# A second substitution on VectorE, held loads, and expert 1's splits on GpSimd

## The chip, the cores and the metric
The kernel runs on one core of one Trainium2 chip. The metric is the device time of one execution in microseconds (us). The engines are named as in the profile: PE is TensorE, DVE is VectorE, ACT is ScalarE, POOL is GpSimd, and SP issues most of the DMAs.

## What is computed
Two layers run behind each other: a delta-rule attention, and a mixture of eight experts on its output. Cut to what matters:

```python
# attention: B=4 batches, H=8 heads, S=768 tokens, D=48
k_n = k / (norm(k) + 1e-6); state = 0
for t in range(S):
    y[:,:,t] = q[:,:,t] @ state
    v_old    = k_n[:,:,t] @ state
    state   += beta[:,:,t] * outer(k_n[:,:,t], v[:,:,t] - v_old)
# experts: x = y as (4, 768, 384), E=8, F=1024
for each batch, token s:
    fresh = argmax(x[s] @ w_gate)
    e = fresh if s == 0 or sigmoid(x[s] @ w_local) < 0.5 else the expert of token s-1
    out[s] = softmax(x[s] @ w_gate)[e] * (relu(x[s] @ w1[e]) @ w2[e])
```

## The kernel before
**Attention.** The 768 tokens are cut into 12 chunks of 64, and two chunks make a macro m (six of them). The recurrence inside a chunk is turned into matrix products and one triangular inverse. `K(n)` loads keys and queries of chunk n (`KQ`, buffers of the pool W) and makes the Gram products in four groups on PE into two PSUM tiles (`pt`). Each group is evacuated by ACT and DVE (L208 to L211) into `gt` (one buffer for the whole kernel, the input of the inverse), `G2` (four buffers) and `amp`.

`T_(m)` makes the inverse for a macro. DVE prepares it: transposes of `gt` into L (L218), norms, and scaling of L in two halves (L232). Then comes the **substitution**: 31 steps, in each a product `fg<-L,X` (L241) and a subtraction `X<-X,fg` (L242), of (31-j)(j+1) elements on each of 128 partitions. All 31 steps of all six macros run on POOL. At the end DVE transposes X into TT (L249) and TX (L252). L and X have two buffers each, TT and TX one.

`Tc(n)` uses the inverse for chunk n: a product of TT with G2 on PE, its copy QQ (L264), a product of QQ with TX, and the matrix XT, which ACT writes in parts (L258, two copies of half the partitions each at L272, and L273). It also loads the values `kv` (768 KB a chunk, three buffers) and DVE scales them (L276). `online(n)` carries the state from chunk to chunk: products on PE with evacuations between them, the output y (L313), its store to HBM and a DMA transpose, and the product with the gate's weights, which ends in the logits `lg` (L326, L330).

**Experts.** `Moe` finds the expert of each token in two routings, z=0 over the first SP=20 of 24 steps, z=1 over the rest; each is a chain of small DVE operations with a few matmuls between. Token lists then gather rows of `xs` by indirect DMAs on POOL. Expert 0 runs in two pieces, the first with LOT=256 tokens from z=0. Weights are split into two f16 parts: the high part on ACT (`whi`, L431), the low one on DVE (`wlo`, L433) or, if the planner chooses so, on POOL by two operations. `weights` does this for experts 0 and 1 in the planned part, `rest` for the others in an order written out by hand. Up products (L448), down products (`downm`, L455), and for each tile of up to 128 tokens a scaling (`yo`, L456) and a scatter to the output follow.

**What sets the order.** Each operation of the attention, the routing and experts 0 and 1 is registered with `add(...)`, with what it reads and writes, the engines that may run it (`e=`) and a cost in ns (`c=`). `Sched` then puts the operations in one order by list scheduling: it takes the ready operation with the longest chain behind it, and a buffer of a pool is given in the order in which the buffers were asked for. What is late on the chip doesn't change this order, as each engine works its list from top to bottom. `boost` raises the priority of operations; `links` lets an operation count as if it waited for another one, for its priority alone; `pre` is a true predecessor.

Of the kernel before, what the change touches and what calls it, by code (L numbers as in the profile page):

```python
# [120 lines left out]
class Attn:  # L121
# [37 lines left out]
    def build(s,extra=(),pre={},post=None):  # L159
# [27 lines left out]
        def K(n):
# [3 lines left out]
            for g in range(2):  # L191
                for j in range(2): add(lambda g=g,j=j:nc.sync.dma_start(KQ[g].t[D(j)].rearrange("r a t -> r (a t)"),s.kq_[n,g,j]),p=[KQ[g]],e='S',c=196608); s.kl[n]=S.ops[-1]; S.ops[-1].pre.update([s.kl[1]] if n==2 else ())
            if cc==0:
                M["b"]=s.bt(); M["gt"]=s.gt()
                add(lambda:nc.sync.dma_start(M["b"].t,s.beta[m]),w=[M["b"]],e='S',c=16384)
            gt=M["gt"]
            for g in range(2):
                for c in range(2):
# [696 lines left out]
```

## Time and profile before

| | us |
|---|---|
| median of three runs | 585.5 (584.71 to 587.43) |
| the profiled execution's own time | 586.47 |
| its span | 584.8 |
| PE busy in it | 459.1 |
| DVE busy | 329.3 |
| POOL busy | 285.9 |
| ACT busy | 210.6 |

The span runs from the first to the last instruction that the profiler saw; the execution's own time includes what lies around it. Busy shares are means over stages that are bound by different engines, so they are read by stage. In a row of a timeline stand the start, the duration, the engine, the line, the operation and its tiles, and in brackets how long the engine had been idle and which engine's work ended that.

### The profile page before, as it was taken

What the parts mean: (1) busy time and instruction counts of PE and PEld (TensorE: products, weight loads), DVE (VectorE), ACT (ScalarE), POOL (GpSimd) and SP (SyncE); (2) the same over time, 40 slices, a digit from 0 to 9 for tenths busy, and PEclk for the clock granted to TensorE, in tenths of its full rate; (3) what the DMA queues carried; (4) which work ended last, traced back from release to release, by engine and by line L of the source; (5) the groups of instructions that cost most, each with busy time, mean ns of one, the idle gap of its engine ahead of it and who ended that gap; (6) DMA issues with size and microseconds to landing.
All of it is one profiled execution on the core that took longest, in us unless ns stands there. A gap on an engine that the chain in (4) does not pass through costs nothing. (4 is left out here: it accounts for less than half of the span.)

```text
span 584.8 us, 18802 instructions
## 1 busy us (share of the span) xinstructions
PE 459.1 (79%) x8119; PEld 351.9 (60%) x8119; DVE 329.3 (56%) x722; ACT 210.6 (36%) x346; POOL 285.9 (49%) x492
## 2 busy tenths in 40 slices
PE   4660277788998887985863489999999999999992
PEld 4550267787987887885862357545565555555551
DVE  3656226547448458233486834852858685868550
ACT  2330254454644755535313211520505141426110
POOL 4089888888888897882001421032233232322301
PEclk9999999577577598586555579999999999999997
DMA  8990001624654455453056372351474656575300
GB/s 224 215 188 1 0 3 58 161 46 129 165 106 106 142 147 165 86 112 57 4 110 244 79 157 94 117 179 48 123 200 126 171 172 174 152 213 151 90 13 25
DMA packets 63668, 69.47 MB, mean 119 GB/s; under 512 B 42931, under 2 KB 54255, under 8 KB 63584
## 3 DMA queue, kind: packets, MB, share of 16 engines
q1 hardware_dynamic: 60032, 58.20, 39.6%
q0 software_dynamic: 3552, 10.06, 5.7%
q8 instruction: 64, 1.05, 0.8%
q14 instruction: 20, 0.16, 0.1%
HBM read 49.49 MB, written 10.05 MB: 102 GB/s over the span
## 5 line engine op out<-in xcount | busy, mean ns | idle before, releaser
L242 POOL TENSOR_TENSOR X<-X,fg 128x31 f32<-128x31 f32 (+15 forms) x186 | 109.8, 590 | 14.6
L241 POOL TENSOR_TENSOR fg<-L,X 128x31 f32<-128x31 f32 (+15 forms) x186 | 98.4, 529 | 16.0 <-DVE X L231 1.6
L167 PE MATMUL pt<-W 48*64 48x128 f32 x768 | 64.1, 374 | 22.6 <-DVE gt L210 13.6
L167 PEld LDWEIGHTS pt<-W 48*64 48x64 f32 x768 | 55.3, 193 | 27.3 <-DVE gt L210 16.3
L448 PEld LDWEIGHTS <-W 128*128 128x128 f16 x432 | 43.7, 102 | 33.4 <-issue 6.9
L448 PE MATMUL pt<-kv,W 128*128 128x384 f16 (+3 forms) x288 | 61.5, 346 | 0.9 <-DVE ft L450 0.7
L450 DVE TENSOR_SCALAR ft<-pt 128x384 f32<-128x384 f32 (+6 forms) x72 | 40.1, 557 | 22.6 <-ACT W L449 14.6
L167 PE MATMUL pt<-TT,G 32*32 32x32 f32 x768 | 24.3, 229 | 31.8 <-DVE TT L249 30.8
L211 DVE TENSOR_TENSOR amp<-pt,mask 128x256 f32<-128x256 f32 x48 | 20.2, 422 | 50.1 <-ACT gt L208 30.9
L449 ACT ACTIVATE W<-pt 128x256 f16<-128x256 f32 (+4 forms) x28 | 12.2, 437 | 85.5 <-PE pt L448 84.1
L167 PEld LDWEIGHTS pt<-TT,G 32*32 32x32 f32 x768 | 22.5, 139 | 33.0 <-issue 27.2
L433 DVE SCALAR_TENSOR_TENSOR W<-W,W 128x768 f16<-128x768 f32 (+1 forms) x33 | 35.9, 1093 | 10.1 <-ACT W L431 9.9
L455 PEld LDWEIGHTS <-W 128*128 128x128 f16 (+2 forms) x272 | 28.0, 103 | 21.9 <-issue 6.4
L438 POOL DMA_INDIRECT out_dram<-y,so x9 | 11.2, 1246 | 55.2 <-DVE y L456 52.8
L436 POOL DMA_INDIRECT G<-xs,gi x25 | 26.6, 1066 | 22.2 <-PE pt L612 12.6
L167 PE MATMUL kps<-R,xtp 64*64 64x48 f32 x704 | 35.6, 281 | 0.7 <-issue 0.7
L449 ACT ACTIVATE xtp<-pt 128x384 f16<-128x384 f32 (+4 forms) x28 | 14.7, 526 | 56.0 <-PE pt L448 43.9
L167 PEld LDWEIGHTS kps<-R,xtp 64*64 64x64 f32 x704 | 34.4, 200 | 0.9 <-issue 0.7
L431 ACT ACTIVATE W<-W 128x768 f16<-128x768 f32 (+1 forms) x33 | 30.2, 935 | 10.7 <-DMA W<-in_moe_w_dram 8.2
L208 ACT ACTIVATE gt<-pt,ma 128x128 f32<-128x128 f32 x48 | 22.4, 479 | 27.1 <-PE pt L167 18.6
L438 POOL DMA_INDIRECT out_dram<-kf,so x7 | 7.9, 1124 | 49.1 <-DVE kf L456 27.0
L455 PEld LDWEIGHTS <-amp 128*128 128x128 f16 (+2 forms) x224 | 22.6, 101 | 14.6 <-issue 0.9
(307 smaller groups left out, 944.1 us busy)
## 6 DMA issues: line engine op xcount, KB each, us to landing
W<-in_moe_w_dram SPq DMA_DIRECT2D x24, 512.0 KB
W<-in_moe_w_dram SPq DMA_DIRECT2D x28, 384.0 KB
W<-in_kq_dram SPq DMA_DIRECT2D x48, 192.0 KB
kv<-in_kv_dram SPq DMA_DIRECT2D x12, 768.0 KB
xs<-y SPq DMA_DIRECT2D x48, 96.0 KB
amp<-in_moe_w_dram SPq DMA_DIRECT2D x3, 384.0 KB
G<-xs,gi POOLq DMA_INDIRECT x25
kv<-G SPq DMA_TRANSPOSE x25
```

Source lines behind the costliest of these rows:

```text
L167: mm=lambda o,l,r,st,sp,tp:MM(o,l,r,start=st,stop=sp,skip_group_check=True,tile_position=tp)
L208: add(lambda go=go,gv=gv:nc.scalar.activation(go(),gv()[:,:,0:32],AF.Copy,scale=s.ma[:,0:1]),r=[ps,"mask"],w=[key],claim=[gt],e='A',c=ca(128))
L211: add(lambda gv=gv,n0=n0:nc.vector.tensor_tensor(am.t[:,n0:n0+4,:],gv()[:,:,64:128],s.mask.unsqueeze(1).to_broadcast([128,4,64]),op=ALU.mu ...
L241: eng.tensor_tensor(tv,l[:,j,j+1:].unsqueeze(2).to_broadcast([128,n,k]),x[:,j,x0:x1].unsqueeze(1).to_broadcast([128,n,k]),op=ALU.mult)
L242: eng.tensor_tensor(x[:,j+1:,x0:x1],x[:,j+1:,x0:x1],tv,op=ALU.subtract)
L431: if e in (None,s.nc.scalar): s.nc.scalar.mul(o,i,256.0)
L433: def wlo(s,st,w,k): s.nc.vector.scalar_tensor_tensor(s.wv(w,k)[:,1],s.wst(st,k),256.0,s.wv(w,k)[:,0],op0=ALU.mult,op1=ALU.subtract)
L436: return s.nc.gpsimd.indirect_dma_start(out=x[0:m],out_offset=None,in_=s.xs[0:nt,:],in_offset=bass.IndirectOffsetOnAxis(ap=ix[0:m],axis=0) ...
L448: for k in range(3): s.nc.tensor.matmul(ps,s.wv(W[k],k)[:,a,0,128*f:128*f+128],xT[:,3*b+k,:],start=(x==0 and k==0),stop=(x==2 and k==2))
L449: def uphi(s,h,ps): s.nc.scalar.activation(h,ps,AF.Relu,scale=2.0**-6)
L450: def upt(s,t,ps): s.nc.vector.tensor_scalar(t,ps,0.0,2.0**-6,op0=ALU.max,op1=ALU.mult)
L455: s.nc.tensor.matmul(po[0:m],h(a,f)[:,c:c+m],s.wv(W[k],k)[:,b,f%2,:],start=(x==0 and f==0),stop=(x==2 and f==7))
```

## The change
It has six parts:
1. **ONV=(1,)**: macro 1's substitution has its 31 steps on DVE, the other five macros theirs on POOL. The costs of both in the planner are new numbers.
2. **The hold**: a copy of one element on POOL from the last keys of chunk 1 into the first `kv` buffer stands ahead of all loads of `kv` and of keys of chunks 2 and up in the planner's order.
3. The constants for the routing (POOL and DVE) are registered behind the scaling of macro 0's L, so they come later; the square root's table on ACT is asked for first.
4. XT's full-width copies: one instead of two halves, and both kinds of XT copies from TT may run on ACT or DVE.
5. The first routing takes SP=18 steps, its priority is 0.4e4 for 0.8e4, and expert 1's low parts are split on POOL alone; its loads no longer wait for the last transpose of y.
6. `down2`: a tile of at most 64 tokens (one of 64, one of 32) has each down matmul of 384 columns as two of 192 at column positions 0 and 64 of PE.

```diff
-    NKV=3; NW=15; NAMP=6; NXT=3; NLX=2; NGT=1; NUS=2; SPLIT=(0,0,0,0,0,0)
+    NKV=3; NW=15; NAMP=6; NXT=3; NLX=2; NGT=1; NUS=2; ONV=(1,)
...
-        for f,e,c in extra: add(f,e=e,c=c,w=["consts"])
...
-  ... s.kl[n]=S.ops[-1]; S.ops[-1].pre.update([s.kl[1]] if n==2 else ())
+  ... s.kl[n]=S.ops[-1]; S.ops[-1].pre.update([s.held] if n>1 else ())
+            if n==1:
+                h=s.kv0=s.kv(); add(lambda:nc.gpsimd.tensor_copy(h.t[0:1,1,0:1],KQ[1].t[0:1,0,0:1]),r=[KQ[1]],w=[(h,1)],claim=[h],e='G',c=200); s.held=S.ops[-1]
...
-            M=mac[m]; L=s.L(); ... a=s.SPLIT[m]
+            M=mac[m]; L=s.L(); ... a=32 if m in s.ONV else 0
...
-  add(fm,r=[(L,j//16)],...,e='VG'[p],c=400+2.4*n*k if p==0 else 450+3.5*n*k)
+  add(fm,r=[(L,j//16)],...,e='VG'[p],c=300+3.2*n*k if p==0 else 590+3.85*n*k)
                     if p:
-                        if j==0 and m: S.links.append((s.lastfm,S.ops[-1]))
+                        if j==0 and m>1: S.links.append((s.lastfm,S.ops[-1]))
...
+            add(lambda e:(e.copy if e is nc.scalar else e.tensor_copy)(XT.t[:,:,32:64],tt()),r=[TT],w=[(XT,1)],claim=[XT],e='AV',c=dict(A=1070,V=700))
             for q in range(2):
-                o,o2=slice(64*q,64*q+32),slice(64*q+32,64*q+64)
-                add(lambda o2=o2:nc.scalar.copy(XT.t[o2,:,32:64],tt()[o2]),r=[TT],p=[XT],e='A',c=ca(512))
...
-            add(lambda:nc.sync.dma_start(kv.t...,s.kv_[n]),w=[kv],e='S',c=786432)
+            add(lambda:nc.sync.dma_start(kv.t...,s.kv_[n]),w=[kv],e='S',c=786432); S.ops[-1].pre.add(s.held)
...
+                if m<0:
+                    for f,e,c in extra: add(f,e=e,c=c,w=["consts"]); S.ops[-1].pre.add(s.scaled)
...
-    SP=20; LOT=256
+    SP=18; LOT=256
...
+    def down2(s,po,h,W,c,m,y,pv):
+        for f in range(8):
+            k=3+f//2
+            for x,(a,b) in enumerate(((0,0),(0,1),(1,0))):
+                for g in range(2):
+                    s.nc.tensor.matmul(po[64*g:64*g+m,0:192],h(a,f)[:,c:c+m],s.wv(W[k],k)[:,b,f%2,192*g:192*g+192],...,tile_position=(0,64*g))
+        s.nc.scalar.copy(y[0:m,192:384],po[64:64+m,0:192])
+        s.nc.vector.tensor_scalar(y[0:m,0:192],po[0:m,0:192],pv[0:m],2.0**-26,...)
+        s.nc.vector.tensor_scalar(y[0:m,192:384],y[0:m,192:384],pv[0:m],2.0**-26,...)
...
-  add(lo,r=[CK,w],w=[st],...,e='VG',c=dict(V=cv(n),G=2*cg(n))); S.ops[-1].pre.update(aft[1:] if aft else ())
+  add(lo,r=[CK,w],w=[st],...,e='G' if aft else 'VG',c=dict(V=cv(n),G=2*cg(n))); S.ops[-1].pre.update(aft[:1] if aft else ())
...
-                for o_ in S.ops[i_:]: o_.boost=0.8e4
+                for o_ in S.ops[i_:]: o_.boost=0.4e4
...
+                if m>64:
+                    s.downm(...); s.yo(y,po,s.pv[:,a:a+1],m)
+                else: s.down2(po,lambda z,f:h(z,f,n),W[e],128*j,m,y,s.pv[:,a:a+1])
```

Besides, the buffers of L and X join the pool W when the attention ends, and the Gram groups are linked, for their priority, to evacuations of earlier ones.

The new order is shown at three places. The first is DVE between the preparation of macro 1 and the transposes of macro 0. L1 and X1 belong to macro 1, X0 and TT0 here to macro 0, and amp and gt are evacuations of Grams. Before, the end of the preparation is followed by the transposes:

```order
L232 TENSOR_TENSOR L1_118<-L1_118,mm0_108 128x512
L231 COPY X1_120<-mm0_108 128x32
L232 TENSOR_TENSOR L1_118<-L1_118,mm0_108 128x512
L228 STREAM_TRANSPOSE nT1_107<-nn0_105 128x32
L276 TENSOR_TENSOR kv2_102<-kv2_102,nT1_107 128x768
L249 STREAM_TRANSPOSE TT0_121<-X0_119 128x256 x4
L252 STREAM_TRANSPOSE TX0_122<-X0_119 128x256 x4
```

In the changed kernel, 25 of the 31 steps of macro 1 (25 products and 25 subtractions) stand there, and these are the last of them:

```order
L244 TENSOR_TENSOR fv_123<-L1_118,X1_120 128x207
L245 TENSOR_TENSOR X1_120<-X1_120,fv_123 128x9x23
L279 TENSOR_TENSOR kv1_101<-kv1_101,nT0_106 128x768
L244 TENSOR_TENSOR fv_123<-L1_118,X1_120 128x192
L245 TENSOR_TENSOR X1_120<-X1_120,fv_123 128x8x24
L244 TENSOR_TENSOR fv_123<-L1_118,X1_120 128x175
L245 TENSOR_TENSOR X1_120<-X1_120,fv_123 128x7x25
L252 STREAM_TRANSPOSE TT0_121<-X0_119 128x256 x4
L255 STREAM_TRANSPOSE TX0_122<-X0_119 128x256 x4
L233 MEMSET X0_119 128x1024
L214 TENSOR_TENSOR amp4_95<-pt1_147,mask_74 128x256
```

Two kv scalings have moved in among the steps, half of L's scaling has too, and the transposes TT have moved behind them; steps 25 to 30 stand among the evacuations that follow.

The second place is POOL at the end of macro 0's substitution. Before, macro 1's first step follows at once:

```order
L241 TENSOR_TENSOR fg_124<-L0_117,X0_119 128x31
L242 TENSOR_TENSOR X0_119<-X0_119,fg_124 128x31
L241 TENSOR_TENSOR fg_124<-L1_118,X1_120 128x31
L242 TENSOR_TENSOR X1_120<-X1_120,fg_124 128x31
L241 TENSOR_TENSOR fg_124<-L1_118,X1_120 128x60
```

In the changed kernel, 30 small rows of constants follow macro 0's last step, and behind the last of them comes macro 2, which uses the buffers L0 and X0 again:

```order
L398 MEMSET kp0_172 128x32
L398 MEMSET kp1_173 128x32
L399 MEMSET vals_171 32x24 x4
L234 COPY X0_119<-mm0_108 128x32
L244 TENSOR_TENSOR fg_124<-L0_117,X0_119 128x31
L245 TENSOR_TENSOR X0_119<-X0_119,fg_124 128x31
```

POOL's next work behind macro 0 is thus macro 2, and its first step waits for macro 2's preparation on DVE.

The third place is POOL behind the last substitution. Before, the gathers of z=1 (G2) stand right behind the one-hot copies and the count (L661):

```order
L436 DMA hz0_128<-xs_57,gi_179 128x768
L436 DMA hz1_129<-xs_57,gi_179 128x768
L657 COPY oh_175<-oh0_209 128x8x20
L657 COPY oh_175<-oh1_211 128x8x4
L661 TENSOR_TENSOR y1_135<-oh_175,ps_186 128x192
L436 DMA G20_113<-xs_57,gi_179 128x768
L436 DMA G21_114<-xs_57,gi_179 128x768
```

In the changed kernel, splits of expert 1 (L486) stand around that count:

```order
L486 TENSOR_TENSOR W5_81<-W4_80,W5_81 128x1024
L672 COPY oh_175<-oh0_209 128x8x18
L672 COPY oh_175<-oh1_211 128x8x6
L676 TENSOR_TENSOR y1_135<-oh_175,ps_186 128x192
L486 TENSOR_TENSOR W6_82<-W6_82,c256_168 128x1024
L486 TENSOR_TENSOR L0_117<-W6_82,L0_117 128x1024
L486 TENSOR_TENSOR L1_118<-L1_118,c256_168 128x1024
L486 TENSOR_TENSOR X0_119<-L1_118,X0_119 128x1024
L486 TENSOR_TENSOR X1_120<-X1_120,c256_168 128x768
L486 TENSOR_TENSOR W7_83<-X1_120,W7_83 128x768
L442 DMA G20_113<-xs_57,gi_179 128x768
L442 DMA G21_114<-xs_57,gi_179 128x768
```

One split (two operations) has come in ahead of the one-hot copies, three between the count and the gathers, and the last three stand behind the gathers.

More of the change, by code (lines that the diff above doesn't have):

```diff
@@ L182, in build @@
         add(wsp,r=["wc0","wc1"],w=["wc"],c=300)
-        for f,e,c in extra: add(f,e=e,c=c,w=["consts"])
-        s.kl={}; ch=[{} for _ in range(N)]; mac=[{} for _ in range(NM)]
+        s.kl={}; s.grams=[]; s.outs=[]; ch=[{} for _ in range(N)]; mac=[{} for _ in range(NM)]
         KV=lambda t:t.rearrange("p (u q z) t -> p u q z t",u=4,q=2)
@@ L191, in K @@
             for g in range(2):
-                for j in range(2): add(lambda g=g,j=j:nc.sync.dma_start(KQ[g].t[D(j)].rearrange("r a t -> r (a t)"),s.kq_[n,g,j]),p=[KQ[g]],e='S',c=196608); s.kl[n]=S.ops[-1]; S.ops[-1].pre.update([s.kl[1]] if n==2 else ())
+                for j in range(2): add(lambda g=g,j=j:nc.sync.dma_start(KQ[g].t[D(j)].rearrange("r a t -> r (a t)"),s.kq_[n,g,j]),p=[KQ[g]],e='S',c=196608); s.kl[n]=S.ops[-1]; S.ops[-1].pre.update([s.held] if n>1 else ())
             if cc==0:
@@ L232, in fL @@
             def fL(e,z): l=full(L.t)[:,16*z:16*z+16]; e.tensor_mul(l,l,mu.t.unsqueeze(1).to_broadcast([128,16,32]))
-            for z in range(2): add(lambda e,z=z:fL(e,z),r=[mu,ss],w=[(L,z)],claim=[L],**VG(512))
+            for z in range(2): add(lambda e,z=z:fL(e,z),r=[mu,ss],w=[(L,z)],claim=[L],**VG(512)); s.scaled=S.ops[-1]
             for j in range(31):
@@ L335, in build @@
                 T_(m+1)
+                if m<0:
+                    for f,e,c in extra: add(f,e=e,c=c,w=["consts"]); S.ops[-1].pre.add(s.scaled)
             if m>=0:
                 for n in (2*m,2*m+1):
-                    Tc(n); online(n)
+                    i0=len(S.ops); Tc(n); online(n)
+                    for o in S.ops[i0:]: o.boost=0.*(N-n)
                     if n in pre: pre[n](S,s)
@@ L341, in build @@
             for i in range(2): pool.init[i]=[o for o in src.bufs[-1].ops]
-        for pool in (s.amp,s.xtp):
+        for pool in (s.L,s.X,s.amp,s.xtp):
             s.W.join(pool,[[o for b in pool.bufs for o in b.ops]]*len(pool.tiles))
@@ L603, in graph @@
             add(fv,r=["tb"+Z,"smr"+Z,CK],w=["va"+Z],c=600)
-            r0,r1=(0,SP) if z==0 else (0,NS); nn=r1-r0; obk=[("ob",i) for i in range(0,r1,4)]; oak=["oa0"] if z==0 else ["oa1","oa2"]
+            r0,r1=(0,SP) if z==0 else (0,NS); nn=r1-r0; obk=[("ob",i) for i in [*range(0,SP,4),*range(SP,r1,4)]]; oak=["oa0"] if z==0 else ["oa1","oa2"]
             for part,(c0,c1,vk) in enumerate(((0,3,[]),(3,5,["va0"]+(["va1"] if z else [])))):
@@ L674, in graph @@
         add(lambda:s.oneh(4,8,ta,rhv()),r=["ta","va0","va1",CK],w=[rh],c=900)
-        add(lambda:s.prods(4,8,rhv(),q.t),r=[rh]+[("ob",i) for i in range(0,NS,4)],w=[q],claim=[OB,OB2],e='P',c=24*50)
+        add(lambda:s.prods(4,8,rhv(),q.t),r=[rh]+[("ob",i) for i in [*range(0,SP,4),*range(SP,NS,4)]],w=[q],claim=[OB,OB2],e='P',c=24*50)
         add(lambda:s.finish(4,8,q.t,tq[2]),r=[q],w=["gi2"],c=1500)
@@ L693, in graph @@
         add(lambda:s.oneh(8,20,ta,r2()),r=["ta","va0","va1",CK],w=[rh2],c=2100)
-        add(lambda:s.prods(8,20,r2(),q2.t),r=[rh2]+[("ob",i) for i in range(0,NS,4)],w=[q2],claim=[OB,OB2],e='P',c=24*50)
+        add(lambda:s.prods(8,20,r2(),q2.t),r=[rh2]+[("ob",i) for i in [*range(0,SP,4),*range(SP,NS,4)]],w=[q2],claim=[OB,OB2],e='P',c=24*50)
         add(lambda:s.finish(8,20,q2.t,s.tx),r=[q2],w=["gi3"],c=1500)
```

38 lines of the change are left out of this document (21 added, 17 removed).

## The prediction

> **What bounds the kernel now.** I read the slices of the span first, then the costliest groups, then windows cut at the ends of the substitutions, then the timeline at the places that the change touches. All times are of the profiled execution, whose own time of 586.5 us is its span of 584.8 us and 1.7 us around it; the median of the runs, 585.5 us, lies 1.0 us below it, and I take that off at the end. In the slices GpSimd (POOL) is full from the second to the eighteenth, and the granted clock of TensorE is low just there:
>
> ```profile
> POOL 4089888888888897882001421032233232322301
> PEclk9999999577577598586555579999999999999997
> L242 POOL TENSOR_TENSOR X<-X,fg 128x31 f32<-128x31 f32 (+15 forms) x186 | 109.8, 590 | 14.6
> L241 POOL TENSOR_TENSOR fg<-L,X 128x31 f32<-128x31 f32 (+15 forms) x186 | 98.4, 529 | 16.0 <-DVE X L231 1.6
> ```
>
> These two groups are the six substitutions: 6 x 31 steps of a product and a subtraction, 208 us with nothing between them but their own pitch. The windows below run from one substitution's end to the next (columns: window, length, then busy us of PE, PEld, DVE, ACT, POOL, the granted clock, the DMA share, GB/s):
>
> ```profile
> 0.00:28.65 28.65, 16.01 (x160) 13.62 (x160) 13.90 (x44) 8.93 (x21) 7.59 (x59) 1.00 0.97 220
> 28.65:69.10 40.45, 9.39 (x99) 8.22 (x101) 18.64 (x44) 5.49 (x17) 35.49 (x64) 1.00 0.35 71
> 69.10:107.20 38.10, 28.04 (x714) 26.20 (x715) 19.57 (x45) 17.82 (x32) 33.20 (x62) 0.90 0.10 29
> 226.20:267.40 41.20, 30.58 (x1259) 28.96 (x1256) 16.34 (x34) 18.83 (x23) 36.34 (x62) 0.75 0.49 99
> 267.40:301.70 34.30, 29.23 (x917) 27.98 (x918) 17.61 (x52) 15.76 (x19) 0.00 (x0) 0.50 0.26 50
> 301.70:345.80 44.10, 20.84 (x266) 16.30 (x266) 32.46 (x118) 11.46 (x19) 14.81 (x15) 0.58 0.60 162
> ```
>
> So until 267.4 us POOL's chain sets the time; then TensorE's last online chunks at a clock of 0.50; then routing on VectorE (DVE, 32.5 of 44.1 us); from 345.8 us TensorE's experts. A saving counts where it shortens the stretch that it stands in.
>
> **The start.**
>
> ```profile
> 7.19 1.28 ACT L208 ACT_TABLE_LOAD   x1 [7.19 <-PE pt L167]
> 24.38 0.18 DVE L395 CAST io<-ib 128x54 f32<-128x54 int32 x1
> 25.88 0.35 DVE L222 RECIPROCAL t<-s 128x32 f32<-128x32 f32 x1
> 28.65 0.52 POOL L241 TENSOR_TENSOR fg<-L,X 128x31 f32<-128x31 f32 x1
> 29.23 1.90 DVE L276 TENSOR_TENSOR kv<-kv,nT 128x768 f32<-128x768 f32 x2
> ```
>
> The table load stands between the first Gram and its evacuation; it moves ahead of the Gram: 1.3 us. The constants stand on DVE inside the first preparation, from 24.38 to 25.88; they move behind the first substitution, and I count 1.0 of the 1.5 us, as the reciprocal also waits for ACT. So POOL starts near 28.65 - 2.3 = 26.3 us. In the first window the DMA is busy 0.97, and three loads of 768 KB leave the head of it: at 220 GB/s they took 2.36 MB / 220 = 10.7 us of the transfers. The Grams of chunks 2 and 3 thus have their input earlier. The kv scaling of 1.90 us no longer stands ahead of their evacuations on DVE; I count half of it, since the Gram is awaited beside it.
>
> **The second substitution on DVE.**
>
> ```profile
> 48.65 0.77 POOL L242 TENSOR_TENSOR X<-X,fg 128x256 f32<-128x256 f32 x1
> 47.90 0.19 DVE L224 TENSOR_TENSOR t<-t,ss 128x32 f32<-128x32 f32 x1
> 48.13 0.49 DVE L224 TENSOR_TENSOR t<-t,s 128x32 f32<-128x32 f32 x1
> 50.21 0.69 DVE L232 TENSOR_TENSOR L<-L,mm 128x512 f32<-128x512 f32 x1
> 227.47 1.41 DVE L249 STREAM_TRANSPOSE TT<-X 128x256 f32<-128x256 f32 x4
> 68.45 0.45 DVE L249 STREAM_TRANSPOSE TT<-X 128x256 f32<-128x256 f32 x1 [7.24 <-POOL X L242]
> 69.04 2.02 PE L167 MATMUL pt<-TT,G 32*32 32x32 f32 x64 [25.69 <-DVE TT L249]
> 102.25 0.68 DVE L232 TENSOR_TENSOR L<-L,mm 128x512 f32<-128x512 f32 x1
> 106.55 0.24 POOL L241 TENSOR_TENSOR fg<-L,X 128x31 f32<-128x31 f32 x1
> ```
>
> DVE can begin its steps when half of L is scaled: 50.90 us before, less 2.3 and 0.95, so 47.7. From the rows of 32 and 512 elements a two-input operation of n elements costs 0.16 + 0.00104 n, and 0.05 of pitch; step j has (31-j)(j+1) elements, twice. But 25 of the 31 steps stand on DVE ahead of the transposes of macro 0 (TT) that TensorE waits for, with two kv scalings (0.95 each) and half of L's scaling (0.69) between them. What a step costs while POOL works on macro 0 depends on this:
>
> ```profile
> 248.35 0.63 POOL L241 TENSOR_TENSOR fg<-L,X 128x255 f32<-128x255 f32 x1
> 249.03 0.96 DVE L433 SCALAR_TENSOR_TENSOR W<-W,W 128x768 f16<-128x768 f32 x1 [8.55 <-ACT W L431]
> 249.06 1.46 POOL L242 TENSOR_TENSOR X<-X,fg 128x255 f32<-128x255 f32 x1
> ```
>
> POOL's subtraction of 255 elements, 0.68 us a step earlier in the same trace, took 1.46 beside one DVE operation of 0.96: they took turns. I therefore let one DVE operation through for each POOL operation. POOL's first substitution ended at 68.4, so 39.75 us after its start; from 26.3, and with 1.2 us for the turns that don't fit in POOL's pitch, it ends at 67.3. At 47.7 it is where the first row above stood (48.65 is 20.0 after the start), with 30 operations to go: 30 DVE operations, fifteen steps. Ten steps are left (j = 15 to 24: 2275 elements, 2 x 2275 x 0.00104 + 20 x 0.21 = 8.9 us), the scalings 2.6 and four transposes 1.4: 67.3 + 12.9 = **80.2 us, against 69.04** for the first product with TT. If DVE is not held at all, 25 steps take 4875 x 2 x 0.00104 + 50 x 0.21 = 20.6, and it comes at 47.7 + 20.6 + 2.6 + 1.4 = 72.3. I take the held value, as the row at 249.06 is the same pair of operations.
>
> The Trainium skill, page "SBUF — State Buffer", section "Who interferes with whom", says of the port pair shared by the two engines that "it's an exclusive lock", and that an operation of DVE with two SBUF inputs contends with one of GpSimd that reads SBUF; the trace agrees (1.46 against 0.68). This speaks against moving a substitution beside another: by it the first product comes at 80.2, without it at 72.3.
>
> POOL is free from 67 us on, but macro 2's substitution needs the Grams of chunks 4 and 5, whose buffers come free with the products of chunks 0 and 1. So it hangs on TT, and the 38 us that POOL saves are not saved in time. From the product to the end of macro 2's preparation it was 102.93 - 69.04 = 33.9 us. Two XT copies in halves become one each (2 x 1.0, row 269.05 below: 2.15 for two), and the preparation has POOL idle beside it (the rows at 47.90 and 48.13 are one operation without a wait and with one, 0.3 apart; four such make 1.2, an estimate): 30.7, and POOL starts when half of L is scaled, 0.7 sooner: 80.2 + 30.0 = 110.2, **+3.7 us** against 106.55 (not held: 102.3, -4.2). The six late steps, the constants and chunk 5's evacuations on DVE lie inside these 30 us under TensorE's products; the slower rival is the case where they don't. Behind it four substitutions follow each other as before, so this difference goes through to 267.4. XT copies that now run on DVE, up to eight, may hold POOL: 0 to 2 us, I take **+0.6**, less than one turn of 0.78 us (1.46 - 0.68).
>
> **The tail.**
>
> ```profile
> 267.86 2.02 PE L167 MATMUL pt<-TT,G 32*32 32x32 f32 x64 [5.14 <-DVE TT L249]
> 269.05 2.15 ACT L272 COPY xtp<-TT 32x512 f32<-32x512 f32 x2
> 308.06 0.18 DVE L330 TENSOR_SCALAR lg<-lg 128x18 f32<-128x18 f32 x1
> 313.85 0.19 DVE L531 TENSOR_TENSOR oh<-ib,ei 128x32 f16<-128x32 int32 x1
> 314.46 0.50 POOL L661 TENSOR_TENSOR y<-oh,ps 128x192 f32<-128x192 f16 x1
> 317.46 1.22 DVE L433 SCALAR_TENSOR_TENSOR W<-W,W 128x1024 f16<-128x1024 f32 x1 [0.35 <-ACT W L431]
> 325.35 0.95 DVE L433 SCALAR_TENSOR_TENSOR xtp<-xtp,xtp 128x768 f16<-128x768 f32 x1
> 327.55 1.21 POOL L436 DMA_INDIRECT G<-xs,gi  x1 [12.58 <-PE pt L612]
> L691 POOL TENSOR_TENSOR amp<-ft,amp 128x496 f16<-128x496 f32 x1 | 1.4, 1393 | 1.9 <-ACT amp L449 1.9
> ```
>
> Whole XT copies bring the last logits (308.24, 40.4 after the product) 1.9 us sooner: two copies at 1.0 each. Then seven splits leave DVE, six of them in the chain before the experts: 3 x 1.22 + 3 x 0.95 = 6.5 us off it. They go to POOL as two operations each: from 255 elements at 0.63 and 496 at 1.39, 1024 elements are 2.3 (by 0.0021 a piece and 0.2) to 2.9 us. Three splits, six operations (four of 1024, two of 768), stand on POOL between the last one-hot count (L661) and the gathers, 13 to 16 us, I take 14; before, the gathers came 327.55 - 314.96 = 12.6 us behind that row. With six turns of 0.2 lost to DVE: 15.2, so the gathers come 2.6 us later after it; less 1.9, **+0.7**. DVE's saving is covered by this queue. If the queue cost nothing, the tail would gain 1.9 + 6.5 = 8.4; if the first split's two operations too stand across the chain, it loses 0.6 + 4.7 = 5.3. 18 steps in the first routing for 20, and two more in the last one, move 32-wide operations to 48 (0.02 us each by the slope): nothing.
>
> **The small tiles.**
>
> ```profile
> L455 PE MATMUL yps<-W,W 128*32 128x384 f16 x16 | 3.4, 327 | 0.0
> L455 PE MATMUL yps<-L,amp 128*64 128x384 f16 x12 | 2.1, 326 | 0.0
> ```
>
> Two tiles, of 32 and 64 tokens, have 24 matmuls each of 384 columns, by these rows 0.18 to 0.21 us each: 4.2 to 5. In two column halves side by side they last half: 2.1 each, less 0.4 for the added copy and scaling: **-3.4** for both (0, if the halves don't run side by side, to -4.2).
>
> **The sum:** +3.7 + 0.6 + 0.7 - 3.4 = +1.6; 586.5 + 1.6 = 588.1 on the profiled execution, **587.1 us** against the median of 585.5.
>
> **The rivals.** A measurement of this kernel tells about 0.5% from no change, so 582.6 to 588.4 is "same".
> - *DVE gets through between POOL's operations.* For it: the 0.69 us at 50.21 is what 512 elements cost also with POOL idle, while POOL waited. Against it: 249.06. Macro 2 starts at 102.3: 587.1 - 7.9 = 579.2. Chance 0.21.
> - *POOL's splits hold nothing*, since DVE's chain is shorter by them and the gathers wait for TensorE: the tail is -8.4 for +0.7: 578.0. For it: DVE is busy 32.5 of 44.1 us there. Against it: POOL's order puts the splits ahead of the gathers. Chance 0.13; with the one above 0.05, at 570.
> - *DVE becomes the bound between the two substitutions* (slower). After the first TT it still has the TX transposes, eight evacuation pairs, six steps, TT of macro 1, copies and constants ahead of macro 2's preparation, near 20 us. If they come in between TensorE's products instead of under them, the 30 us become 38: 587.1 + 8 = 595. It decides from a first step of macro 2 later than 111.5 (1.3 more, 588.4 in all). Chance 0.19.
> - *The change doesn't do what it says*: the column halves of the small tiles run one behind the other, 587.1 + 3.4 = 590.5. Chance 0.04.
> - My forecast: 0.38, of it 0.28 inside "same", 0.04 below, 0.06 above.
>
> Faster: 0.04 + 0.21 + 0.13 + 0.05 = 0.43. Same: 0.28. Slower: 0.06 + 0.19 + 0.04 = 0.29. The range reaches from 571, a little above the case with both gains, which it leaves out, to the slower rival with the 2 us that XT copies may cost, 597.
>
> **What would show it.** POOL idle from about 67 to 110 us; before 67 us the DVE operations of the substitution at POOL's pitch of 0.7 to 0.8 us, and after it at 0.3 to 0.5; the first product with TT at 80 (72 if not held); the first POOL operation of macro 2 at 110 (102, or 115 and more); the last substitution's end at 271. In the routing stretch, gathers of expert 1 some 15 us behind the last one-hot count, and DVE operations with two inputs waiting up to 2.3 us. The two tiles in 2 us each. A product with TT before 75, or gathers less than 12 us behind L661's place, would make the forecast wrong on the fast side; a first step of macro 2 behind 113, on the slow one.

## The result, and the profile after

The changed kernel takes 605.3 us, the median of four runs (598.4 to 607.3; two more took 602.3 and 608.1), against 585.1 us: a ratio of 1.031 (1.024 to 1.039). Ratios leave out runs more than 1.5% above the fastest of their kernel. It is **slower**, and lies outside the range of the prediction. Its profiled execution is its fastest: 598.4 us with a span of 596.7 us, 11.9 us over the span before. The account below places these 12 us; the other runs of the changed kernel took up to 9.7 us more, at a mean granted clock of 0.811 to 0.838, where the profiled one had 0.837.

The slices of the span and the costliest groups of the changed kernel, as they were shown before:

```profile
POOL 1288600588888997983014674223414141413201
PEclk9999999755589777557555568999999999999997
L245 POOL TENSOR_TENSOR X<-X,fg 128x31 f32<-128x31 f32 (+15 forms) x155 | 90.3, 583 | 12.2
L244 POOL TENSOR_TENSOR fg<-L,X 128x31 f32<-128x31 f32 (+15 forms) x155 | 85.6, 552 | 13.0 <-DVE X L234 1.0
```

POOL does 32 us less in these groups (175.9 for 208.2) and has a hole of two slices before the second run of full ones; that run ends later than before all the same. Windows of the changed kernel, cut at the ends of the substitutions and at the last macro's product (columns as before):

```profile
0.00:26.21 26.21, 16.07 (x160) 13.67 (x160) 12.99 (x34) 8.29 (x23) 3.07 (x16) 1.00 0.97 202
64.45:108.80 44.35, 29.64 (x736) 28.35 (x736) 35.02 (x97) 17.80 (x33) 6.45 (x44) 1.00 0.06 20
108.80:150.10 41.30, 34.73 (x922) 32.68 (x920) 18.80 (x45) 12.20 (x26) 34.64 (x63) 0.54 0.48 101
232.30:274.40 42.10, 36.46 (x1312) 35.17 (x1312) 18.85 (x35) 15.09 (x20) 36.33 (x62) 0.60 0.53 116
274.40:282.90 8.50, 4.39 (x167) 3.94 (x162) 7.22 (x27) 1.65 (x3) 0.00 (x0) 0.58 0.56 97
282.90:317.00 34.10, 29.25 (x803) 27.31 (x804) 16.79 (x56) 11.43 (x16) 2.99 (x3) 0.50 0.21 53
```

The first substitution starts at 26.21 (26.3 was forecast). Macro 2's starts at 108.8, 2.3 us later than before (3.7 forecast), and the last one ends at 274.4, 7.1 us later. The row of 8.5 us is new: before, half a microsecond lay between POOL's last step and the product of the last macro. In it PE is busy for 4.4 us and DVE for 7.2.

The timeline of the changed kernel where DVE and POOL work on two substitutions at once, then at the first product with TT and at the start of macro 2:

```profile
47.03 0.68 POOL L245 TENSOR_TENSOR X<-X,fg 128x255 f32<-128x255 f32 x1
47.05 0.73 DVE L244 TENSOR_TENSOR fv<-L,X 128x60 f32<-128x60 f32 x1
47.78 0.61 POOL L244 TENSOR_TENSOR fg<-L,X 128x252 f32<-128x252 f32 x1
47.81 0.66 DVE L245 TENSOR_TENSOR X<-X,fv 128x60 f32<-128x60 f32 x1
88.68 0.22 DVE L244 TENSOR_TENSOR fv<-L,X 128x60 f32<-128x60 f32 x1
75.15 1.42 DVE L252 STREAM_TRANSPOSE TT<-X 128x256 f32<-128x256 f32 x4
108.04 0.70 POOL L234 COPY X<-mm 128x32 f32<-128x32 f32 x1 [36.94 <-DVE mm L229]
116.33 0.96 POOL L233 MEMSET X<- 128x1024 f32 x1 [1.92 <-DVE TX L255]
```

The same 60 elements take DVE 0.22 us with POOL idle and 0.73 beside it: one DVE operation for each POOL operation, while POOL keeps its own 0.6 to 0.7. The first product follows at 76.7. The last row is one that I had not priced: the clearing of X for macro 3 now stands on POOL amid macro 2's steps. POOL waits 1.92 us for a transpose of macro 1 that frees X, then clears for 0.96, and the chain stops for 2.9 us.

The timeline of the changed kernel behind POOL's last step:

```profile
276.32 0.65 PE L329 MATMUL pt<-wc,xt 128*32 128x9 f16 x33 [1.54 <-issue]
276.90 1.96 PE L167 MATMUL yps<-S,W 48*64 48x48 f32 x64
279.21 0.18 DVE L531 TENSOR_TENSOR kp<-kp,rs 128x18 f32<-128x18 f32 x1
280.31 0.58 PE L539 MATMUL pt<-sc,blk 128*128 128x18 f32 x2 [1.45 <-DVE sc L540]
281.46 1.42 DVE L252 STREAM_TRANSPOSE TT<-X 128x256 f32<-128x256 f32 x4
281.76 0.88 PE L329 MATMUL pt<-wc,xt 128*32 128x18 f16 x48 [0.86 <-DMA xt<-y]
282.93 2.01 PE L167 MATMUL pt<-TT,G 32*32 32x32 f32 x64 [0.29 <-DVE TT L252]
```

The product of the last macro, from which 314 us are left to the end of the span, now stands on PE behind the logits of chunks 8 and 9 (L329) and behind a matmul of the first routing (L539). On DVE the transposes TT stand behind that routing's first seventeen operations. Before, PE had the product ahead of these logits, and it ran at 267.86. So the 12 us are: +2.3 at macro 2's start, +3.0 in macro 2, +1.8 to the end of the last substitution, +8.0 from there to the product, and -3.1 behind the product.

### The profile page after: what moved, and what is told of

Read it like the earlier page. It is cut to its first block, busy times and chain, and to the rows that moved or that the text cites. A ratio compares the mean times of both kernels' runs of the same rounds, so it can differ in the third digit from the quotient of the medians.

```text
span 596.7 us, 18911 instructions
## 1 busy us (share of the span) xinstructions
PE 465.6 (78%) x8167; PEld 359.2 (60%) x8167; DVE 365.0 (61%) x785; ACT 188.3 (32%) x326; POOL 284.2 (48%) x449
## 5 line engine op out<-in xcount | busy, mean ns | idle before, releaser
L245 POOL TENSOR_TENSOR X<-X,fg 128x31 f32<-128x31 f32 (+15 forms) x155 | 90.3, 583 | 12.2
L244 POOL TENSOR_TENSOR fg<-L,X 128x31 f32<-128x31 f32 (+15 forms) x155 | 85.6, 552 | 13.0 <-DVE X L234 1.0
L167 PE MATMUL pt<-W 48*64 48x128 f32 x768 | 66.4, 384 | 22.1 <-DVE gt L213 12.1
L454 PEld LDWEIGHTS <-W 128*128 128x128 f16 x360 | 37.5, 105 | 28.0 <-issue 5.5
L167 PEld LDWEIGHTS pt<-TT,G 32*32 32x32 f32 x768 | 22.4, 137 | 40.9 <-issue 39.9
L461 PEld LDWEIGHTS <-W 128*128 128x128 f16 (+2 forms) x324 | 32.4, 100 | 22.0 <-issue 2.0
L455 ACT ACTIVATE amp<-pt 128x384 f16<-128x384 f32 (+5 forms) x36 | 17.6, 489 | 82.7 <-PE pt L454 32.9
L316 DVE SCALAR_TENSOR_TENSOR y<-yps,y 128x768 f16<-128x768 f32 x12 | 11.4, 948 | 38.0 <-ACT y L315 38.0
L439 DVE SCALAR_TENSOR_TENSOR W<-W,W 128x768 f16<-128x768 f32 (+1 forms) x25 | 27.6, 1106 | 10.0 <-ACT W L437 9.1
L455 ACT ACTIVATE W<-pt 128x384 f16<-128x384 f32 (+5 forms) x36 | 17.8, 495 | 49.6 <-PE pt L454 41.7
L454 PE MATMUL pt<-kv,xtp 128*128 128x416 f16 (+2 forms) x96 | 29.0, 342 | 0.5 <-DVE ft L456 0.4
```

Of the source, the lines that this page charges most:

```text
L167: mm=lambda o,l,r,st,sp,tp:MM(o,l,r,start=st,stop=sp,skip_group_check=True,tile_position=tp)
L244: eng.tensor_tensor(tv,l[:,j,j+1:].unsqueeze(2).to_broadcast([128,n,k]),x[:,j,x0:x1].unsqueeze(1).to_broadcast([128,n,k]),op=ALU.mult)
L245: eng.tensor_tensor(x[:,j+1:,x0:x1],x[:,j+1:,x0:x1],tv,op=ALU.subtract)
L316: add(lambda:nc.vector.scalar_tensor_tensor(y.t[:,:,1,:],py.t[:,:,0:384],256.0,y.t[:,:,0,:],op0=ALU.mult,op1=ALU.subtract),r=[py,(y,0)],w= ...
L439: def wlo(s,st,w,k): s.nc.vector.scalar_tensor_tensor(s.wv(w,k)[:,1],s.wst(st,k),256.0,s.wv(w,k)[:,0],op0=ALU.mult,op1=ALU.subtract)
L454: for k in range(3): s.nc.tensor.matmul(ps,s.wv(W[k],k)[:,a,0,128*f:128*f+128],xT[:,3*b+k,:],start=(x==0 and k==0),stop=(x==2 and k==2))
```

## The experiments

Each figure of time is a median with the ratio to the kernel before on the same chip; e9 is a single run. In the cuts of code, `...` stands for what is left out.

**e1: TT of the last macro planned ahead of the first routing.** The edit makes the routing's first reduction a successor of the four transposes:

```diff
+            s.ttops=S.ops[-4:]
...
-            add(lambda sl=sl:V.tensor_reduce(mx[:,sl],...),r=[*lgk,CK],w=["mx"+Z])
+            add(lambda sl=sl:V.tensor_reduce(mx[:,sl],...),r=[*lgk,CK],w=["mx"+Z]); S.ops[-1].pre.update(A.ttops)
```

> Only edit to the changed kernel: the first routing is planned behind the last macro's transposes TT. Theory A (VectorE's order: TT stands behind the head of the first routing, and from the substitution's end at 274.4 us to TT at 281.5 us 7.1 us are lost): the first product of the last macro comes at 275 to 276 us where it came at 282.9, and the time falls by 6 to 7 us. Rival B (TensorE's own backlog: it has online work of chunk 8 to do until about 279 us): the product comes at 278 to 280 us wherever TT stands, and the time falls by 3 to 4 us or less. If neither place counts, no change.

597.3 us, 1.027 (1.021 to 1.033), which overlaps with the changed kernel's 1.031. TT comes 2.1 us sooner, and the product 2.1 us later. The timeline of e1:

```profile
279.37 1.41 DVE L252 STREAM_TRANSPOSE TT<-X 128x256 f32<-128x256 f32 x4
284.17 0.88 PE L330 MATMUL pt<-wc,xt 128*32 128x18 f16 x48 [3.79 <-DMA xt<-y]
284.98 2.01 PE L167 MATMUL pt<-TT,G 32*32 32x32 f32 x64
```

PE had the logits in its queue ahead of the product, and these waited 3.8 us for a DMA transpose of y. With DVE's hold gone, PE's order holds the product as long, and neither expectation came true. The new constraint changed the planned order on DVE from 209 us on, so this is not a move of TT alone.

**e2: all substitutions on GpSimd, the rest as changed.**

```diff
-    ... NUS=2; ONV=(1,)
+    ... NUS=2; ONV=()
-                        if j==0 and m>1: S.links.append((s.lastfm,S.ops[-1]))
+                        if j==0 and m: S.links.append((s.lastfm,S.ops[-1]))
```

> Only edit to the changed kernel: macro 1's substitution is on GpSimd again (ONV empty), all other parts stay. Theory C (the substitution on VectorE is the root: TT of macro 0 waits behind 25 steps on VectorE, 7.7 us, and TensorE never makes that up): first product with TT at 66 to 67 us, last substitution's end at 264 to 266 us, and the time 578 to 582 us, faster than the kernel before by the earlier start (2.3 us) and the small tiles (3.4 us). Rival D (the other parts, the splits on GpSimd and the early first routing, cost as much): 585 us or more.

618.9 us, 1.063 (1.057 to 1.068), slower still. Macro 2's steps end sooner than in the changed kernel (143.65), but POOL then waits 5.8, 11.8 and 11.5 us ahead of macros 3, 4 and 5, and the last product comes at 307.6. A window of e2:

```profile
187.00:237.00 50.00, 42.45 (x1120) 40.02 (x1120) 23.12 (x55) 19.60 (x36) 33.30 (x63) 0.52 0.34 94
```

PE is busy for 42.5 of these 50 us, at a clock of 0.52; POOL is not the bound. Undoing this part did not bring back the order of before: the planner made another one on every engine. At the last macro it is worse than the changed kernel's: POOL's last step ends at 290.6, and the product stands 17.0 us behind it; 6.1 us of that are six splits of weights that now stand on DVE between the first and the second of the four transposes TT. So e2 doesn't price the substitution on DVE by itself.

**e3: X cleared for macro 3 on DVE.**

```diff
-            add(lambda e:e.memset(X.t,0.0),...,e='GV',c=dict(G=1000,V=1150))
+            add(lambda e:e.memset(X.t,0.0),...,e='V' if m==3 else 'GV',c=dict(G=1000,V=1150))
```

> Only edit to the changed kernel: the clearing of X for macro 3 is on VectorE, not on GpSimd in the middle of macro 2's substitution, where it waited 1.9 us for VectorE and took 1.0. Theory E (GpSimd's chain still sets the time there): macro 2's substitution takes 38.4 us where it took 41.3, and the time falls by 2 to 3 us. Rival B (TensorE's backlog sets it): GpSimd's chain ends 2.9 us earlier, and the time falls by less than 1 us.

594.6 us, 1.020 (1.017 to 1.023). Macro 2 is 3 us shorter as expected. Then the planner put another small operation in the same place one macro later; POOL in e3:

```profile
184.44 0.76 POOL L234 COPY X<-mm 128x32 f32<-128x32 f32 x1 [9.37 <-DVE mm L229]
```

POOL waits 9.4 us for DVE amid macro 3's steps, and the last product comes at 290.7. The stall is confirmed as a mechanism. Its worth in whole time is not settled: the ratio is 1.1 points lower than that of the changed kernel, but the last product comes 7.8 us later, the profiled run is as long (597.8 us for 598.4), and the order is another one.

**e4: the kernel before with macro 1's steps on DVE, planned anew.**

```diff
-    ... NUS=2; SPLIT=(0,0,0,0,0,0)
+    ... NUS=2; SPLIT=(0,32,0,0,0,0)
```

> The kernel before with one edit: macro 1's substitution on VectorE, at the planner's old costs. Then some 10 steps stand ahead of TT of macro 0, not 25. Theory C (what hurts is TT waiting behind the steps): TT comes at 68 to 71 us, within 2 us of the kernel before, macro 2's substitution starts at 100 to 104 us (106.55 before), and the time is 581 to 586 us. Rival F (a substitution on VectorE beside GpSimd hurts by their turns wherever TT stands): macro 2 starts behind 107 us and the time is 588 us or more.

614.2 us, 1.053 (1.049 to 1.056). Here, too, the planner changed all the rest: macro 2 starts at 121, and the last product comes at 297.4. Like e2 it shows how much hangs on the order, and does not price the part.

**e5: the changed kernel with the last product ahead of chunk 8's logits**, by a successor added after the ranking, so that the order on DVE and ACT is the same up to the end of the last substitution, and differs from there on:

```diff
-        s.rank(); E={...}; ...
+        s.rank()
+        for a,b in s.late: b.pre.add(a); a.succ.append(b)
+        E={...}; ...
...
+            if n==10: S.late.append((S.ops[-1],s.lf[8]))
```

> The changed kernel with one constraint on the planned order: the first product with TT of the last macro (chunk 10) stands on TensorE ahead of the logits of chunk 8, as in the kernel before, where it now stands behind the logits of chunks 8 and 9 and the first routing's product. The order up to there is the same row by row. Theory H (this place in TensorE's order costs the 8.5 us from the substitution's end at 274.4 us to the product at 282.9): the product comes 1.5 to 3 us behind the end of the last substitution, and the time falls by 5 to 8 us, to 1.018 to 1.023 of the kernel before. Rival G (TensorE at half clock has as much work in front of the last logits whatever the order): the product comes earlier, the last logits do not, and the time stays within 3 us of 605.

593.5 us, 1.018 (1.014 to 1.022). The timeline of e5 at POOL's last step and the product:

```profile
275.37 0.25 POOL L247 TENSOR_TENSOR X<-X,fg 128x31 f32<-128x31 f32 x1
277.96 1.96 PE L169 MATMUL yps<-S,W 48*64 48x48 f32 x64 [0.24 <-DVE y L319]
280.15 2.02 PE L169 MATMUL pt<-TT,G 32*32 32x32 f32 x64 [0.24 <-DVE TT L254]
```

The gap is 4.5 us for 8.5, and the time falls by 1.3 points of the ratio. So the order at the last macro carries a good part of the loss. The gap stays 4 us above that of before: PE is at online products of an earlier chunk (the second row) until just before TT is there, where before it had waited 5.1 us for TT.

The product itself comes only 2.8 us sooner than in the changed kernel (280.15 for 282.93); more is gained behind it. These windows run from the product to the last logits, in the changed kernel, in e5 and in e11 (below), which has e5's order there:

```profile
282.93:322.40 39.47, 32.91 (x864) 29.82 (x865) 17.76 (x60) 12.81 (x17) 7.21 (x6) 0.50 0.28 67
280.15:312.20 32.05, 24.47 (x924) 23.39 (x925) 20.08 (x70) 11.26 (x15) 0.71 (x1) 0.66 0.36 68
282.53:317.30 34.77, 28.70 (x926) 27.44 (x926) 19.71 (x69) 10.87 (x15) 0.70 (x1) 0.50 0.30 60
```

At the same clock of 0.50, the order of e5 and e11 takes 4.7 us less than that of the changed kernel; the other 2.7 us of e5 go with its clock of 0.66.

**e6: e5, and the set-up of X (clearing, copy) on DVE in the later macros.**

```diff
-            add(lambda e:e.memset(X.t,0.0),...,e='GV',c=dict(G=1000,V=1150))
-            add(lambda e:e.tensor_copy(X.t[:,0:1024:33],mu.t),...,e='VG',c=dict(V=460,G=300))
+            add(lambda e:e.memset(X.t,0.0),...,e='V' if m>1 else 'GV',c=dict(G=1000,V=1150))
+            add(lambda e:e.tensor_copy(X.t[:,0:1024:33],mu.t),...,e='V' if m>2 else 'VG',c=dict(V=460,G=300))
```

> As the run above, and the clearing of X and the copy into X for macros 3 to 5 are on VectorE alone, so that GpSimd has nothing but steps between its substitutions. Theory E (GpSimd's chain sets the time up to the last macro; the clearing cost 2.9 us in it): each of the four last substitutions takes 38 to 41 us with gaps of at most 1.5 us, the last ends 2 to 4 us earlier than in the run above, and so does the kernel. Rival B (TensorE's backlog): GpSimd waits before its substitutions instead, and the time is that of the run above within 1.5 us.

594.4 us, 1.017 (1.014 to 1.020), the same as e5, as rival B had it. No set-up stands amid POOL's steps any more, and macro 2 ends at 145.0. But POOL then waits 2.8, 3.0 and 9.8 us ahead of macros 3 to 5. A window of e6:

```profile
232.00:275.00 43.00, 39.87 (x1261) 38.62 (x1264) 22.99 (x49) 17.93 (x29) 29.61 (x48) 0.50 0.44 107
```

What POOL saves becomes a wait: PE is busy for 39.9 of 43 us, at a clock of 0.50.

**e7: the first TT ahead of step 14 of macro 1 on DVE, with e6's set-up, without e5's edit.**

```diff
...
+                    s.st[m,j]=S.ops[-1]
...
+            if m==0: s.tt0=S.ops[-1]
+            if m==1: S.late.append((s.tt0,s.st[1,14]))
```

> The changed kernel with TT of macro 0 planned ahead of step 14 of macro 1 on VectorE (14 steps ahead of it, not 25), and X's clearing and copy on VectorE as above. Theory C (TT behind the steps is the root): the first product comes at 67 to 69 us (76.7), macro 2's substitution starts at 98 to 103 us (108.8), and the time falls to 583 to 590 us. Rival I (from there on TensorE's pace sets the time, with its clock near half): macro 2 starts as early, but GpSimd waits 3 us or more ahead of macros 3, 4 or 5, and the time is 594 us or more.

601.8 us, 1.030 (1.026 to 1.035): no gain. The first product with TT comes at 68.1 and macro 2's steps at 102.1, both sooner than in the kernel before. POOL then waits 8.9, 5.5 and 3.9 us, and the last product comes at 284.7. So making up the late first product gains nothing by itself. At the last macro e7 has the old order again, though its first routing has 18 steps too; the product and the logits of chunk 8 in e7, where POOL's last step ends at 283.52:

```profile
284.71 1.99 PE L169 MATMUL pt<-TT,G 32*32 32x32 f32 x64
293.84 0.88 PE L334 MATMUL pt<-wc,xt 128*32 128x18 f16 x48
```

The product stands 1.2 us behind the last step and 9 us ahead of these logits. So the 18 steps and the changed loads do not by themselves force the order that cost 8 us in the changed kernel.

**e8: the kernel before with the column halves of the small tiles** (`down2` and its call, as in the change).

> The kernel before with the small tiles in column halves alone; the order ahead of them is the same. Theory (halves run side by side): two tiles in 2.0 to 2.5 us each where they took 3.9 to 5, and the time falls by 3 to 4 us (ratio 0.993 to 0.995). Rival: one behind the other, no change.

579.6 us, 0.992 (0.990 to 0.995), a gain of some 4.5 us. The end of the 64-token tile on PE in the kernel before, then in e8:

```profile
465.87 2.11 PE L455 MATMUL yps<-L,amp 128*64 128x384 f16 x12
```

```profile
462.43 1.16 PE L462 MATMUL yps<-L,amp 128*64 128x192 f16 x24
```

Twice as many matmuls, each half as wide, take half the time; each tile takes 2.2 us for 4.1. The two halves run side by side.

**e9: the kernel before with less work on GpSimd.** It leaves out steps 9 to 20 of the substitutions of macros 2 to 5, the order being kept:

```diff
                     def fm(...):
+                        if m>1 and 9<=j<21: return
```

> The kernel before with twelve of the 31 steps (j = 9 to 20, the long ones) left out in macros 2 to 5, so that part of the inverse is not computed; the order of all that is left is the same. GpSimd has 17 us less to do in each of four substitutions. Theory B (TensorE's pace through online work and Grams sets the time of the attention, with only some 5 us of slack against GpSimd, the idle time ahead of its last product with TT): that product comes at 258 to 264 us, where it came at 267.9, and GpSimd waits before its substitutions instead. Rival J (GpSimd's chain sets it, as the prediction had it): it comes 40 us or more sooner, before 230 us. The whole time is not to be read, as the tokens' experts change with the data.

577.3 us, against a median of 583.4 for the kernel before. POOL's busy time falls from 285.9 to 219.8 us, by 66; the last substitution ends at 247.4 instead of 267.3, but the last product comes only 6.5 us sooner, at 261.33. POOL's first steps of macros 3, 4 and 5 in e9, the first part of the product, and a window:

```profile
142.67 0.53 POOL L242 TENSOR_TENSOR fg<-L,X 128x31 f32<-128x31 f32 x1 [16.18 <-DVE X L231]
181.69 0.53 POOL L242 TENSOR_TENSOR fg<-L,X 128x31 f32<-128x31 f32 x1 [18.72 <-DVE X L231]
224.87 0.53 POOL L242 TENSOR_TENSOR fg<-L,X 128x31 f32<-128x31 f32 x1 [20.40 <-DVE X L231]
261.33 0.62 PE L167 MATMUL pt<-TT,G 32*32 32x32 f32 x16
184.00:226.00 42.00, 37.68 (x1199) 36.17 (x1200) 26.50 (x56) 23.95 (x40) 19.01 (x35) 0.71 0.55 142
```

The 16 to 20 us that a macro loses on POOL come back as a wait for the next preparation, while PE, whose order is that of before, is busy for 37.7 of 42 us. This is the decisive run: in the kernel before, POOL is full from 28 to 267 us, and yet with a quarter of its work gone the last product came only 6.5 us sooner. What then holds the preparations is PE with the evacuations of its products: in e9 the preparation of macro 3 begins on DVE at 137.9, right behind the last evacuation of the Grams.

**e10: the kernel before, in its own order, with macro 1's steps sent to DVE.** The planner still counts them as POOL's; only the engine differs:

```diff
+                    if m==1: eng=nc.vector
-                    def fm(...,tmp=(s.fv,s.fg)[p]):
+                    def fm(...,tmp=s.fv if m==1 else s.fg):
```

> The kernel before with macro 1's steps given to VectorE in the places of the old order that they had on GpSimd, so no other instruction changes its place on any engine, and TT of macro 0 stays ahead of them. Theory B: macro 2's substitution starts at 100 to 104 us, 3 to 6 sooner than 106.5, and the time changes by 0 to -3 us, since TensorE's order and pace are those of the kernel before. Rival F (a substitution on VectorE holds up the evacuations that TensorE waits for, wherever it stands): the second product with TT and the Grams come later, macro 2 starts behind 107 us, and the time is 588 us or more.

588.3 us, 1.008 (1.005 to 1.011). Neither expectation holds whole: macro 2 starts at 104.5, 2.0 us sooner, yet the time is that of rival F. But macro 1's own transposes come late, and POOL then waits 5.0, 1.9 and 3.2 us ahead of macros 3 to 5. The two products that waited for TT, in e10:

```profile
117.57 2.01 PE L167 MATMUL pt<-TT,G 32*32 32x32 f32 x64 [1.25 <-DVE TT L250]
274.44 1.99 PE L167 MATMUL pt<-TT,G 32*32 32x32 f32 x64 [2.19 <-DVE TT L250]
```

This is the price of the part in an order that it did not change: near 5 us, and 3 to 6 by the interval.

**e11: e5, with expert 1's splits on DVE or POOL as before.**

```diff
-            add(lo,...,e='G' if aft else 'VG',...)
+            add(lo,...,e='VG',...)
```

> The run with the product first (593.5 us), and expert 1's low parts on VectorE or GpSimd as the planner chooses, so that the splits leave GpSimd's queue in the routing; the order up to the last logits is that run's. Theory K (splits on GpSimd hold VectorE's two-input operations 1.1 to 2.1 us each and the gathers): the time falls by 2 to 5 us. Rival L (VectorE's relief pays for the turns): no change within 1.5 us, or slower.

Median 587.6 us of ten runs (579.9 to 649.8), ratio 1.001 (0.997 to 1.005); the plain medians give 1.007. From the last product to the end of the span it takes 303.2 us for e5's 307.7, 4.5 less, though at a lower clock (0.815 for 0.853). From the last logits to the gathers it takes 18.8 us for 22.0: in e5 POOL begins the gathers right behind a split, in e11 it waits for PE. So the splits on POOL cost some 4.5 us by the profiles, 0.9 to 1.7 points by the ratios.

**e12: the kernel before in its own order, with the parts that need no new order:** the small tiles' halves, the table load first, DVE's constants behind the first scaling, one whole XT copy for two halves.

```diff
-                add(lambda o2=o2:nc.scalar.copy(XT.t[o2,:,32:64],tt()[o2]),...)
+                add(lambda q=q:nc.scalar.copy(XT.t[:,:,32:64],tt()) if q==0 else None,...)
...
-        for o,x in s.order():
+        out=s.order(); a=[t for t in out if t[0] in s.first]; out=a+[t for t in out if t[0] not in s.first]
+        i=[k for k,t in enumerate(out) if t[0] is s.mark][0]; a=[t for t in out[:i] if t[0] in s.ex and t[1]=='V']; out=[t for t in out[:i+1] if t not in a]+a+out[i+1:]
+        for o,x in out:
```

> The kernel before with what helped, each in the old order: the small tiles in halves, the square root's table loaded first, VectorE's constants behind macro 0's preparation, and one whole XT copy on ScalarE for two halves. The substitutions stay on GpSimd. Expected from the parts: -4.2 for the tiles as measured, -2.4 for the first step at 26.2 us, -1 to -2 for the copies in the tail: 574 to 578 us, ratio 0.983 to 0.99. If TensorE's pace swallows the earlier start: 579 to 580.

574.1 us, 0.985 (0.982 to 0.988): faster than both kernels. The first substitution starts at 26.24, as in the changed kernel and without its hold of the loads, and the last product in e12 comes 3.4 us sooner than before:

```profile
264.51 2.01 PE L169 MATMUL pt<-TT,G 32*32 32x32 f32 x64 [2.64 <-DVE TT L253]
```

## Why the prediction was wrong, point by point

- **The start** was right: 26.2 for 26.3. In e12 it is worth having, together with the XT copies: 0.7 points more than e8.
- **The turns on the port** were right for DVE: one operation for each of POOL's. The size was not: the first product came at 76.7, halfway between 80.2 (held) and 72.3 (not held). POOL's first substitution was not 1.2 us longer beside DVE, as I took it, but took 38.2 us for 39.8, so the hold ended sooner. (A slip of mine lies in it too: 47.7 is 21.4 us after 26.3, not 20.0, so 28 of POOL's operations were left and not 30.) From the product to macro 2's start it took 32.1 us for my 30.0. So the +2.3 for +3.7 at macro 2 is near in part by luck, since the two misses offset each other.
- **"Behind it four substitutions follow each other as before, so this difference goes through to 267.4"** failed. From macro 2's start to the last substitution's end it lost 4.8 us more, where I took +0.6; 2.9 of them are the clearing in POOL's queue; the rest, 1.9, is within the 0 to 2 us that I had given the XT copies, and by what it comes is not shown. I had looked at what each part moves at three places, and not at what the new plan put among POOL's later steps. That the stall is there is shown (macro 2 lost 3 us by it, and in e3 not); that its removal helps the whole is not, as e3 and e6 gave the time back in waits at later macros.
- **The product of the last macro** is the largest miss, 8.0 us. My sum lets the tail begin at the product as before, half a microsecond behind POOL's last step, and of the new routing it says "18 steps in the first routing for 20 ... nothing". That priced the width of the operations and not their place. In the new plan the routing's head on DVE, and the logits of chunks 8 and 9 and a routing product on PE, stand ahead of the last macro's product. e1 shows that moving TT on DVE does not bring the product forward; e5 moves PE's product and halves the gap. Which part of the change brings this order is open. With 18 steps (two a chunk) the routing needs the logits up to chunk 8, where 20 needed chunk 9's, so it can stand earlier; but e7 has the 18 steps, the loads and the costs of the change, and there the product stands 1.2 us behind POOL's last step.
- **"So until 267.4 us POOL's chain sets the time"** was true to 6.5 us only (e9). This did not cause the miss, but it fits what the other runs showed: in e2, e6, e7 and e10 POOL gained time and then waited 2 to 12 us ahead of later substitutions for their preparation.
- **The tail** was right in direction, and mis-sized. The gathers came 62.1 us after the product for 59.7 before, +2.4 where I took +0.7: 0.9 of the 1.9 came from the logits, and the splits cost 3.3 for 2.6. In e11 their removal gave 4.5. POOL's operations were cheaper than I thought (1.9 to 2.1 us for 1024 elements, for 2.3 to 2.9), but the wait was not for them. The changed kernel ahead of the gathers:

```profile
331.21 1.89 POOL L486 TENSOR_TENSOR L<-L,c 128x1024 f32<-128x1024 f32 x1
331.31 1.83 DVE L617 CAST vals<-tb 128x6 f16<-128x6 f32 x1
333.18 2.14 POOL L486 TENSOR_TENSOR X<-L,X 128x1024 f16<-128x1024 f32 x1
333.25 2.11 DVE L681 SCALAR_TENSOR_TENSOR rs<-ei,ri 128x24 f32<-128x24 int32 x1
345.03 1.07 POOL L442 DMA_INDIRECT G<-xs,gi  x1 [6.54 <-DVE gi L739]
```

POOL is done with the splits at 345.03 - 6.54 = 338.5 and waits 6.5 us for DVE's list. It is DVE's short chain that was held, operation by operation, until POOL's long one had ended. I took six turns of 0.2 for that. There were six, but they took 9.4 us together, where the same six take 1.0 in the kernel before and 1.1 in e11, which has no splits on POOL. The cast in e11:

```profile
322.63 0.18 DVE L620 CAST vals<-tb 128x6 f16<-128x6 f32 x1
```

- **The small tiles** were right: -3.4 forecast, about -4.5 in e8.
- **The slower rival** that I named (DVE the bound between the two substitutions, macro 2 later than 111.5) did not come: macro 2 started at 108.8. The loss came by mechanisms that I had not named. That the sum, +1.6, had the right sign is luck: the time went up by terms that I had put at 0.6 and at nothing.

For the profiled execution the misses add up: -1.4 at macro 2's start, +4.2 behind it, +8.0 at the last macro, -0.4 behind the product, 10.4 in all, and 588.1 + 10.4 = 598.5. The medians differ by 20 us instead of 12. The other runs of the changed kernel had, but for one (0.838, 602 us), lower granted clocks (0.811 to 0.824, 605 to 608 us). In e11 time and clock go together too: 579.9 us at 0.871, 587.7 at 0.835, 590.5 at 0.831, though also 587.4 at 0.815. Why the clock is lower in some runs, and whether the new order makes this more frequent, stays open.

Taken apart by ratios: e10 (1.008) and e8 (0.992) together give 1.000, which is where e11 stands. But e12 has the start and the XT copies besides e8's part, which are worth 0.7 points there (0.992 to 0.985), and e11 has them too; so by these ratios as much is lost again in its order, and where is not told apart. What lies between e11 and the changed kernel is the splits (0.9 to 1.7) and the order at the last macro (1.3 points).

## What to carry to other kernels

A full engine is not yet a bound with room above it: before moving work off it, shorten that work in the old order (as e9 does) and see how soon the next engine takes over: 66 us less on POOL brought 6.5 here. Where a planner makes the order, price a change by what the new order puts ahead of the work that all wait for, on every engine's queue, and test its parts in the old order, since a replanned kernel is another kernel. Small operations in a queue are dear by their place: a clearing of 0.96 us cost 2.9, a copy of 0.76 us 10.1, and a cast of six elements 1.8.

## What the hardware showed that I had not expected

Six small DVE operations beside POOL's splits lasted until POOL's running operation ended (within 0.05 us), however small they were, and two of them have one input in SBUF: the cast of 6 elements above took 1.83 us beside POOL's 1.89, and 0.18 in e11. Not every operation was held: a reduction of 192 elements took 0.60 us beside POOL's 2.12, and 0.61 in the kernel before. The Trainium skill, page "SBUF — State Buffer", section "Who interferes with whom", says that casts can enter a mode that uses the shared ports; the trace agrees, and shows that the price is what is left of POOL's operation and not the length of DVE's own.

TensorE's granted clock stayed near half in stretches in which it was hardly idle: in e6 it was 1.00 from 184 to 194 us and 0.50 from there to 286 us, with PE busy for 83.4 of these 92 us, and no gap of PE from 184 to 286 us was longer than 2.1 us. The Trainium skill, page "TensorE: Matmul & The Clock Gate", section "HAM oscillation — how this bites in real kernels", names idle gaps over about 3.4 us as what lowers the clock; this stretch differs from that rule, and no run here shows what lowered the clock.
